# Grouped-query attention on one core: the last pair's transposes, the last V's split and the last norm

## Chip, core and metric

The kernel runs on one core of a Trainium2 chip. The metric is device time in microseconds, the median of several executions. A core has five engines that work side by side, each on its own list of instructions: TensorE (PE, matmuls and transposes), VectorE (DVE), ScalarE (ACT), GpSimd (POOL) and SyncE (SP, which here issues every DMA). They wait for one another by semaphores. Data lies in HBM, is worked on in SBUF (128 partitions), and matmuls write to PSUM.

## What is computed

```python
B, Hq, Hkv, Sq, Sk, D = 16, 32, 8, 16, 2048, 128      # all bfloat16

def reference(q, k, v):
    rep = Hq // Hkv                                    # 4
    k = jnp.repeat(k, rep, axis=1)
    v = jnp.repeat(v, rep, axis=1)
    scores = jnp.einsum("bhqd,bhkd->bhqk", q, k) * D ** -0.5
    p = softmax(scores, axis=-1)
    return jnp.einsum("bhqk,bhkd->bhqd", p, v)
```

Four query heads share one K and V head, so for each of 16 x 8 = 128 groups (batch, KV head) there are 4 x 16 = 64 query rows against 2048 keys. K and V are 64 MB each and are read once.

## The kernel before

Two groups make a **pair**: 64 pairs (NP = 64), each with 128 rows of queries, 1 MB of K and 1 MB of V. For each pair p:

- SP loads K(p) (line 175) and V(p) (line 183), `Kn` and `Vb`. V lies as 128 partitions x 2 groups x 16 blocks (J = 16) of 128 values: partition a holds 16 consecutive keys, so a load has rows of 16 x 128 x 2 bytes = 4 KB. There are 6 K buffers and 8 V buffers. V(63) alone is loaded as two halves of 8 blocks (lines 185 to 188), each with a semaphore of its own, `sem_vl[0]` and `sem_vl[1]`.
- VectorE transposes K (line 311, `KT`).
- TensorE makes the scores S(p) (lines 220 and 264, into `S_ps`, four banks of PSUM).
- VectorE scales them and takes their minimum (line 327, `Sneg`, `nbias`, semaphore `sem_max`), and later the reciprocal of the row sums (line 318, `rrec`, `sem_rec`).
- ScalarE takes the exp (line 357, `P`, with the row sums read from an accumulator, `sem_exp`).
- TensorE transposes P in two stages of four (line 276, `ST_ps`, `sem_st`), each evicted to SBUF by ScalarE (line 367, `PT`, `sem_ev`).
- TensorE multiplies by V: PV(p) (lines 292 and 298, 16 blocks; for the last twelve pairs (NFAST) each block is two matmuls, one for each group, so 32 in all; `sem_pv`). For pairs up to 60 the result goes to `O_ps`; for pairs 61, 62 and 63 into the first 128 columns of three different banks of `S_ps` (`o_ap`, line 145), which the last scores have left by then.
- ScalarE multiplies by the reciprocal and writes the output tile: the norm (lines 380 and 384, `O`, `sem_nm`).
- SP stores it (line 200, 32 KB, 256-byte rows, `sem_o`), one of eight output buffers.

**What sets the order.** TensorE and ScalarE work through two lists written out by hand, `pe_prog` and `act_prog` (lines 92 to 138). In the loop at lines 119 to 128 each step p has the scores of pair p+1, PV and norm of pair p-3 (PVLAG = 3) and the transposes of pair p. What follows the loop (lines 129 to 138) is the tail: TensorE has PV(60), PV(61), PV(62), the transposes of pair 63, PV(63); ScalarE has exp(63), norms 60 and 61, norm 62, the two evictions of pair 63, norm 63. SP's order is the loop at lines 202 to 211: the load of V five steps behind that of K, the store twelve behind, so that V(63) is issued after store(55) and then come stores 56 to 63 alone. At the end SP waits for all stores (line 213).

PV(p) waits for the second eviction of its pair (line 280), for its V (line 282; for pair 63 the two semaphores of the halves, at blocks 0 and 8, line 290), and in the last three pairs for VectorE to have read all scores (line 284). The transposes of a pair wait for its exp (line 271) and for a free stage. The norm waits for PV, the reciprocal and a stored output buffer (lines 373 to 376).

## Time and profile before

| what | value |
|---|---|
| median of 3 runs | 345.48 us (345.41 to 345.74) |
| profiled execution, its own time | 346.02 us |
| its span, from the first instruction to the last | 344.1 us |
| granted TensorE clock, mean | 0.999 of full speed |
| HBM read and written | 136.31 MB and 2.10 MB, 402 GB/s over the span |
| traffic from 332 to 334 us | 383 GB/s |
| traffic from 336 to 337 us | 231 GB/s |
| traffic from 340 to 340.5 us | 34 GB/s |

All times inside the execution are microseconds from the start of the span. The page divides the span into 40 slices of 8.6 us, and gives busy shares by slice as digits (9 is 90% or more). A row of the chain of waits or of the timeline has a start, a length, the engine, the line of the kernel, the operation, and how many instructions it merges; "issue" in the chain is time for which the profile shows no instruction that ended it, which can also be a DMA's landing. A row of DMA issues has what is moved, the queue, the count, the size of each and the time from issue to landing.

### The profile page before, as it was taken

Reading aid. Unit: us, or ns where it says so; the run is one execution under the profiler, and the core shown is the slowest. Engines: PE = TensorE matmul, PEld = TensorE weight load, DVE = VectorE, ACT = ScalarE, POOL = GpSimd, SP = SyncE. Lnnn points to the kernel's source line nnn. Section 1 sums busy time; section 2 is a strip of 40 time slices with the busy share of each in tenths; the row PEclk is TensorE's granted clock in tenths of the full one; section 3 lists DMA queues with packets and bytes.
Section 4 is the critical chain, followed back from the end, with each engine's and each line's share of the span. In section 5 each row is a group of like instructions: output and inputs, shape, how many; then the busy total and the mean of one; then the engine's idle time right before and its main releaser. Section 6 shows DMA issues by size and latency. Waiting matters only on the chain.

```text
span 344.1 us, 8217 instructions
## 1 busy us (share of the span) xinstructions
PE 314.5 (91%) x3904; PEld 189.9 (55%) x2880; DVE 297.4 (86%) x320; ACT 292.3 (85%) x405; POOL 30.3 (9%) x15
## 2 busy tenths in 40 slices
PE   0776999999999999999999999999999999888694
PEld 0422575557555655566566656655665566445263
DVE  2279999999899989998899989998999998988930
ACT  1238899999999999999999999999999999987774
POOL 4500004000400004000210004000040000000000
PEclk9999999999999999999999999999999999999999
DMA  7999999999999999999999999999999999999993
GB/s 292 428 415 416 414 412 416 413 414 413 415 416 417 413 415 416 415 419 416 412 417 415 414 415 417 415 418 417 414 415 420 416 412 416 421 414 415 411 380 97
DMA packets 37300, 138.94 MB, mean 404 GB/s; under 512 B 11408, under 2 KB 11408, under 8 KB 29072
## 3 DMA queue, kind: packets, MB, share of 16 engines
q1 hardware_dynamic: 37264, 138.42, 99.3%
q8 instruction: 27, 0.44, 0.5%
q14 instruction: 9, 0.07, 0.1%
HBM read 136.31 MB, written 2.10 MB: 402 GB/s over the span
## 4 chain that ended last, share of the span: by engine, by line
PE 87%; issue 5%; ACT 3%; DVE 2%; DMA 2%; POOL 1%; SPq 0%; ACTq 0%
PE O_ps L292 28%; PE S_ps L264 18%; PE ST_ps L276 16%; PE S_ps L220 16%; PE ST_ps L242 4%; PE O_ps L298 2%; DMA Qn<-in_q_dram 2%; ACT P L357 1%; DVE KT L311 1%; POOL Q L164 1%; DVE Sneg L327 1%; PE S_ps L298 1%; ACT PT L367 1%; ACT QT L347 0%; ACT O L380 0%
## 5 line engine op out<-in xcount | busy, mean ns | idle before, releaser
L327 DVE TENSOR_SCALAR_CACHE_REDUCE Sneg<-S_ps 128x2048 f32<-128x2048 f32 x64 | 146.3, 2286 | 26.7 <-PE S_ps L220 25.3
L357 ACT ACTIVATE P<-Sneg,nbias 128x2048 bf16<-128x2048 f32 x64 | 158.8, 2482 | 7.5 <-DVE Sneg L327 6.1
L311 DVE STREAM_TRANSPOSE KT<-Kn 128x1024 f32<-128x1024 f32 x128 | 150.9, 1219 | 9.6 <-DMA Kn<-in_k_dram 9.4
L264 PE MATMUL S_ps<-KT,QT 32*64 32x512 bf16 x1024 | 104.3, 395 | 5.2 <-DVE Sneg L327 4.4
L220 PE MATMUL S_ps<-KT,QT 32*64 32x512 bf16 x1024 | 102.9, 389 | 0.0
L292 PEld LDWEIGHTS O_ps<-Vb,PT 128*128 128x128 bf16 x832 | 77.2, 98 | 42.3 <-issue 34.1
L292 PE MATMUL O_ps<-Vb,PT 128*128 128x256 bf16 x832 | 99.9, 273 | 0.0
L367 ACT ACTIVATE PT<-ST_ps 128x512 f32<-128x512 f32 x128 | 69.6, 595 | 7.7 <-PE ST_ps L276 6.5
L276 PE MATMUL ST_ps<-ident,P 128*128 128x128 f32 x512 | 70.0, 280 | 1.9 <-ACT P L357 1.9
L264 PEld LDWEIGHTS S_ps<-KT,QT 32*64 32x64 bf16 x1024 | 30.2, 104 | 71.0 <-issue 62.3
L276 PEld LDWEIGHTS ST_ps<-ident,P 128*128 128x128 f32 x512 | 55.6, 142 | 12.0 <-ACT P L357 7.7
L380 ACT ACTIVATE O<-O_ps,rrec 64x128 bf16<-64x128 f32 x104 | 37.7, 363 | 14.2 <-PE O_ps L292 13.4
L164 POOL COPY Q<-Qn 128x4096 bf16<-128x4096 bf16 x8 | 28.8, 3600 | 224.3 <-PE ST_ps L242 181.5
L242 PE MATMUL ST_ps<-ident,Q 128*128 128x128 f32 x128 | 20.4, 291 | 10.1 <-POOL Q L164 10.1
L347 ACT ACTIVATE QT<-ST_ps 128x512 f32<-128x512 f32 x32 | 19.3, 603 | 10.0 <-PE ST_ps L242 10.0
L242 PEld LDWEIGHTS ST_ps<-ident,Q 128*128 128x128 f32 x128 | 16.4, 151 | 10.1 <-issue 10.1
L298 PE MATMUL O_ps<-Vb,PT 128*64 128x128 bf16 x288 | 9.8, 220 | 7.0 <-issue 7.0
L298 PEld LDWEIGHTS O_ps<-Vb,PT 128*64 128x64 bf16 x288 | 8.5, 110 | 12.7 <-issue 12.7
L318 DVE RECIPROCAL rrec<-rowsum 128x1 f32<-128x1 f32 x64 | 10.1, 158 | 3.1 <-ACT P L357 3.1
L357 ACT ACTIVATION_READ_ACCUMULATOR P<-Sneg,nbias 128x1 f32 x64 | 12.2, 191 | 0.0
L384 ACT ACTIVATE O<-O_ps,rrec 128x128 bf16<-128x128 f32 x9 | 3.3, 367 | 6.7 <-PE O_ps L298 6.7
L298 PE MATMUL S_ps<-Vb,PT 128*64 128x128 bf16 x96 | 3.3, 220 | 2.7 <-issue 1.9
(11 smaller groups left out, 12.3 us busy)
## 6 DMA issues: line engine op xcount, KB each, us to landing
Kn<-in_k_dram SPq DMA_DIRECT2D x64, 1024.0 KB, 15.8
Vb<-in_v_dram SPq DMA_DIRECT2D x63, 1024.0 KB, 17.5
Qn<-in_q_dram SPq DMA_DIRECT2D x8, 256.0 KB, 15.2
out_dram<-O SPq DMA_DIRECT2D x64, 32.0 KB, 15.7
Vb<-in_v_dram SPq DMA_DIRECT2D x2, 512.0 KB, 12.3
```

What stands on the lines that cost most here:

```text
L164: gp.tensor_copy(Q4[:, :, :, :, :].rearrange("p j b r x -> p (j b) r x"), src.unsqueeze(2).to_broadcast([128, 16, 4, 64]),).then_inc(sem_q ...
L220: return pe.add_instruction(mybir.InstMatmult(name=nc.get_next_instruction_name(), engine=mybir.EngineType.PE, ins=[pe.lower_ap(rhs), pe.l ...
L242: ins = pe.transpose(dst[:, 128 * j:128 * (j + 1)], src[:, 4 * x + j, b, :], ident4[:, :])
L264: ins = pe.matmul(s_ap, w, x, start=(acc == 0), stop=(acc == 3))
L276: ins = pe.transpose(dst[:, 128 * t:128 * (t + 1)], P[p % 2][:, 128 * x:128 * (x + 1)], ident4[:, :])
L292: ins = pe.matmul(O_ps[:, 0:256], pt[:, j // 2, j % 2, :], Vb[p % NV][:, :, j, :], start=(j == 0), stop=(j == J - 1),)
L298: ins = pe.matmul(o_ap(p)[64 * g:64 * (g + 1), :], pt[:, j // 2, j % 2, 64 * g:64 * (g + 1)], Vb[p % NV][:, g, j, :], start=(j == 0), stop ...
L311: dve.transpose(KT[p % NKT][:, :].rearrange("p (t b e a x) -> p x e t b a", t=J // 2, b=2, e=2, x=2)[:, x, :, :, :, :], Kn[p % NK][:, :].b ...
L327: dve.tensor_scalar(Sneg[p % 2][:, :].rearrange("p (t h x) -> p h t x", t=8, h=2), S_ps[:, :].rearrange("p (h t x) -> p h t x", t=8, h=2), ...
L357: act.activation(P[p % 2][:, :].bitcast(BF16).rearrange("p (n y e) -> p n y e", n=16, e=2), Sneg[p % 2][:, :].rearrange("p (n e y) -> p n ...
L367: act.activation(PT[p % NPT][:, 4 * h:4 * (h + 1), :].rearrange("p t q -> p (t q)"), stage_ap(u), ACT.Copy,).then_inc(sem_ev, 1)
L380: ins = act.activation(Osb[p % NO][rows, :], O_ps[rows, 128 * g:128 * (g + 1)], ACT.Copy, scale=rrec[rows, p:p + 1])
```

## The change

Three edits, all at the end of the work.

- In the hand-written lists the transposes of pair 63, and so their evictions on ScalarE, come before PV(62) and norm 62.
- V(63) is loaded as blocks 0 to 11 and 12 to 15 instead of 0 to 7 and 8 to 15; PV(63) waits for the second semaphore ahead of block 12.
- The norm of pair 63 leaves ScalarE's list. VectorE does it after its last reciprocal, as a `tensor_scalar` that reads PSUM and writes the same output tile, and signals a new semaphore, `sem_nl`, for which SP's last store waits.

```diff
+LASTV = ((0, 12), (12, 16))
...
+    sem_nl = sem("sem_nl")
...
     for p in range(NP - 4, NP - 2):
         norm(p)
+    transposes(NP - 1)
     pv(NP - 2)
     norm(NP - 2)
-    transposes(NP - 1)
     pv(NP - 1)
-    norm(NP - 1)
...
-                for x in range(2):
-                    dst = Vb[s][:, :, 8 * x:8 * (x + 1), :].rearrange("a g j d -> a g (j d)")
-                    src = vf[:, 2 * p:2 * p + 2, 1024 * x:1024 * (x + 1)]
+                for x, (lo, hi) in enumerate(LASTV):
+                    dst = Vb[s][:, :, lo:hi, :].rearrange("a g j d -> a g (j d)")
+                    src = vf[:, 2 * p:2 * p + 2, 128 * lo:128 * hi]
                     sp.dma_start(dst, src).then_inc(sem_vl[x], 16)
...
             def store(p):
                 s = p % NO
-                sp.wait_ge(sem_nm, p + 1)
+                if p < NP - 1:
+                    sp.wait_ge(sem_nm, p + 1)
+                else:
+                    sp.wait_ge(sem_nl, 1)
...
                     for j in range(J):
-                        if p == NP - 1 and j % 8 == 0:
-                            pe.wait_ge(sem_vl[j // 8], 16)
+                        if p == NP - 1:
+                            for x, (lo, _) in enumerate(LASTV):
+                                if j == lo:
+                                    pe.wait_ge(sem_vl[x], 16)
...
             recip(NP - 1)
+            p = NP - 1
+            dve.wait_ge(sem_rec, NP)
+            dve.wait_ge(sem_o[p % NO], 16 * (p // NO))
+            dve.wait_ge(sem_pv, NP)
+            dve.tensor_scalar(Osb[p % NO][:, :], o_ap(p), rrec[:, p:p + 1], None, op0=ALU.mult).then_inc(sem_nl, 1)
```

## Prediction

> **What bounds the kernel now.** I read the page's head first, then the chain of work that ended last over its closing microseconds, then the timeline of the same stretch, and last the DMA issues of the final loads.

> ```profile
> span 344.1 us, 8217 instructions
> PE 314.5 (91%) x3904; PEld 189.9 (55%) x2880; DVE 297.4 (86%) x320; ACT 292.3 (85%) x405; POOL 30.3 (9%) x15
> DMA  7999999999999999999999999999999999999993
> GB/s 292 428 415 416 414 412 416 413 414 413 415 416 417 413 415 416 415 419 416 412 417 415 414 415 417 415 418 417 414 415 420 416 412 416 421 414 415 411 380 97
> ```

> Three engines are near 90%, but the row of DMA shares is nine in every slice but the first and last: some 415 GB/s, never let go. The loads set the pace, and the change touches only what follows the last of them. So the closing stretch is all that counts. Its chain (start, length, what):

> ```profile
> 334.53 0.36 issue
> 334.89 1.08 PE S_ps L298 x32
> 335.97 1.55 issue
> 337.52 1.08 PE S_ps L298 x32
> 338.61 0.60 PE ST_ps L276 x4
> 339.21 0.02 issue
> 339.23 0.48 ACT PT L367
> 339.71 0.01 issue
> 339.73 0.60 ACT PT L367
> 340.33 0.04 issue
> 340.37 1.10 PE S_ps L298 x32
> 341.48 0.02 issue
> 341.50 0.37 ACT O L384
> ```

> From 334.89 on these are PV(61), PV(62), the transposes of pair 63, their two evictions, PV(63) and its norm. The 1.55 us of "issue" ahead of PV(62) need a name. The timeline (start, length, engine, line) tells what was ready meanwhile:

> ```profile
> 334.08 2.46 ACT L357 ACTIVATE P<-Sneg,nbias 128x2048 bf16<-128x2048 f32 x1
> 336.43 0.20 ACT L357 ACTIVATION_READ_ACCUMULATOR P<-Sneg,nbias 128x1 f32 x1
> 336.78 0.38 ACT L384 ACTIVATE O<-S_ps,rrec 128x128 bf16<-128x128 f32 x1
> 338.54 1.09 PE L276 MATMUL ST_ps<-ident,P 128*128 128x128 f32 x8
> ```

> The exp of pair 63 was done at 336.63, and the transposes that need it started at 338.54. They stood in TensorE's queue behind PV(62), which waited for its V. The issues of the loads, each answered for its own stretch (count, size, us to landing):

> ```profile
> Vb<-in_v_dram SPq DMA_DIRECT2D x1, 1024.0 KB, 14.3
> ```

> ```profile
> Vb<-in_v_dram SPq DMA_DIRECT2D x1, 512.0 KB, 12.2
> ```

> ```profile
> Vb<-in_v_dram SPq DMA_DIRECT2D x1, 512.0 KB, 12.5
> ```

> The first is V(62), issued at 323.09: it landed at 337.4, and PV(62) started at 337.52. The others are the halves of V(63), issued at 326.60 and 327.59: landed at 338.8 and 340.1. So PV(63) at 340.37 was released by the evictions, 0.3 us after its last V. That 0.3 us would look like all there is to gain; but PV(63) also began with all its V on the chip, and could have run most of its matmuls ahead of the last piece.

> **The transposes ahead of PV(62).** Nothing is added or removed, three groups change places. The timeline has the transposes of pair 62 at 332.42, 0.05 us after their exp's accumulator read ended (332.16+0.21); so those of pair 63 start at 336.68, 1.86 earlier. ScalarE has the norms of pairs 60 and 61 in front of the evictions, until 336.78+0.38 = 337.16. The first eviction follows the first transpose by 0.69 (338.54 to 339.23), so starts at 337.37, behind those norms; the pair takes 1.08 and ends at 338.45, and PV(63) may follow 0.06 later, at 338.51. PV(62) pays: a group of eight transposes holds TensorE for 1.02 (from 328.12 to 329.14 where scores follow), so it starts at 337.70 instead of 337.52 and leaves TensorE at 338.72. The norm of pair 62 now queues behind the evictions on ScalarE, which is free at 338.45, before PV(62) ends (338.80): it moves by 0.18, and store(62) on SP with it, from 339.0 to 339.2. Nobody but store(63) queues behind that, some 1.7 us later. So neither ScalarE nor TensorE holds PV(63) past 338.72, where it was 340.37. What is late next is its V.

> **V(63) as 12 and 4 blocks.** Two issues as before, 512 rows as before, of 3 KB and 1 KB instead of 2 KB and 2 KB. The halves landed 1.3 us apart, so a quarter is 0.65: twelve blocks land at 338.8+0.65 = 339.45, the last four at 340.1 as now. Rows of 3 KB and 1 KB occur nowhere in the trace. Its packets took 18 ns for 256 B, 84 for 2 KB, 159 for 4 KB and 309 for 8 KB. One bound: 3 KB as 4 KB and 1 KB as 2 KB, 243 ns where two of 2 KB took 168, over 16 rows for each of the 16 DMA engines +1.2 us. The other: 3 KB as 2 KB, 1 KB as 256 B, 102 ns, -1.1 us. The rows lie on a straight line (75 ns for 2 KB more, 150 for 4 KB more), which gives 121.5+46.5 = 168: no change, which I take.

> [...] The halves here came at 512 KB in 1.3 us, 403 GB/s, beside 415 for whole loads, since they stand in a full queue; I go by the row.

> PV(63) then starts at 339.45+0.08 = 339.53 (PV(62) came 0.1 behind its load). Its 32 matmuls take 1.10, 28 ns each with 0.22 for the last. The 24 of the first twelve blocks are issued by 339.53+0.67 = 340.20, and the last four blocks, landed at 340.1, are usable at 340.18: no second wait worth a number. It ends at 340.63 where it ended at 341.47: **0.84 gained**. If the four blocks come later, all of that goes on at once, less 0.02. Of the 0.84, about 0.2 is the split's: with halves PV(63) would wait at its middle until 340.18 and have 16 matmuls left, 15 x 0.028 + 0.22 = 0.64, ending at 340.82.

> **The norm on VectorE.** Removed: ScalarE's 0.37 (L384). Added: one tensor_scalar of 128x128 out of PSUM with a scalar by partition, and a semaphore of its own. VectorE has done its last reciprocal at 336.67+0.16, so it stands at the wait with nothing behind it. Its other wait, for store(55) (issued at 324.33, 13.3 us to landing), is over at 337.6. The trace has no such instruction. Nearest rows: the reciprocal of 128x1, 158 ns, and the tensor_scalar with reduction of 128x2048 out of PSUM, 2286 ns. 128 columns are near the short one; on the line between them it is 158 + 127 x 1.04 = 290 ns. I take 0.29: **0.08 gained**. The ends are 0.16 (0.21 gained) and 2.29 (1.9 lost).

> [...]

> **The store.** SP issued store(63) at 341.9 as ScalarE's norm ended at 341.87, and it took 1.5 us to land; the span ends 0.7 after that. All of it moves along, to an issue at 340.98 and a landing at 342.5.

> **Sum.** 0.84 + 0.08 = 0.92. The profiled execution took 346.02, with 344.1 of span and 1.92 around it: 343.2 and 345.10. It lies 0.54 above the median of the runs, 345.48; the tail scales by next to nothing, so **344.56**, 0.27% faster.

> **Rivals.**
> *The load hides it.* The time of the chain from V's last byte is what it was: V(63) lands later by some tenths because steady traffic ahead of it shifts. For: the last slices' rate falls to 97 GB/s, so a few laggard DMA engines, not the queue, time the last landing, and that wanders. Against: three runs lie within 0.33 us. With the last piece at 340.5, PV(63) waits until 340.58, then eight matmuls, 7 x 0.028 + 0.22 = 0.42: ends at 341.0, gain 0.47+0.08 = 0.55, **344.9**: no change that can be told.

> *The last store runs into the laggards* (slower). Store(62), issued at 339.0 while V(63) was still landing, took 2.7 us, store(63) on an empty queue 1.5. The latter's issue moves from 1.8 us behind V's last landing to 0.9. If that is near enough to cost 2.7, 1.2 is lost and **345.76** results, slower than now. It decides if the backlog outlasts about 341.4. Against: store(62) had landed by 341.8, and the traffic is down to 5 GB/s from 340.5 to 341 and to none after.

> *Dearer rows* (slower). At the bound above, 3 KB as 4 KB and 1 KB as 2 KB, V(63) ends at 341.3; PV(63) ends at 341.3+0.08+0.42 = 341.8, gain -0.33+0.08: **345.73**. It exceeds the present time once the pieces come 0.9 us later than I say.

> *It does not do what it says.* If PV(62) waited for something other than V(62), the transposes ahead of it still help, but if the exp released late (past 338.5) they don't: gain only 0.08 and the split, **345.2**. The exp's row at 336.63 speaks against.

> **How the numbers follow.** My case 0.70; the load hiding it 0.13; the store 0.07; dearer rows 0.06; the last 0.04. What a measurement here can tell from no change is 0.2%, 0.69 us, so faster means below 344.79 and slower above 346.17. My case by itself spans 344.3 to 344.85, with the VectorE operation from 0.16 to 0.4 and the landing off by 0.2; 0.04 of its 0.70 fall within 0.2%, and 0.02 of the second case beyond: faster 0.68. The slow rivals are priced within 0.2%; a store or rows dearer than that, or a VectorE operation near its long end (346.5), make slower 0.07 of their 0.17, and the rest is same, 0.25. The range takes in the load's case and the last one, and leaves out the slow ones and the long end of VectorE's bound, 0.13 and a little: 344.2 to 345.4.

> **What would show it.** Transposes of pair 63 near 336.7, ahead of PV(62) at 337.7; evictions ended by 338.5; PV(63) starting on the landing of the large piece, near 339.5, with at most 0.1 us of idle time before its 25th matmul; a VectorE tensor_scalar near 0.3 us; store(63) issued near 341.0 with 1.5 us to landing. Wrong would be a last V landing past 340.5, a store of over 2 us, or a norm above 0.4.

## The result, and the profile after

| | kernel before | changed kernel |
|---|---|---|
| median of 22 runs each | 345.67 us (345.29 to 346.01) | 345.04 us (344.40 to 345.51) |
| profiled execution, span | 344.1 us | 343.1 us |

The ratio is 0.9982 with a 95% interval of 0.9975 to 0.9988: 0.63 us, or 0.18%, faster (0.4 to 0.9 us by the interval). That is clear of zero and smaller than the 0.92 us that were predicted. Here the changed kernel's runs also cover more, 1.1 us where those of before cover 0.7; in the experiments below the kernel before covers 1.3 to 2.1. The one profiled execution gained 1.0.

The head of the page after, with its rows of DMA share and rate in 40 slices:

```profile
span 343.1 us, 8217 instructions
PE 312.1 (91%) x3904; PEld 189.2 (55%) x2880; DVE 297.6 (87%) x321; ACT 291.8 (85%) x404; POOL 30.3 (9%) x15
DMA  7999999999999999999999999999999999999993
GB/s 294 429 414 415 415 411 413 414 416 417 412 418 419 413 415 417 412 420 415 412 421 414 414 416 416 415 418 417 415 412 419 419 412 420 417 413 418 410 393 126
```

VectorE has one instruction more, ScalarE one less, and the loads run as they did. The chain of waits over the last ten microseconds (start, length, what):

```profile
326.19 12.98 DMA Vb<-in_v_dram
339.17 0.14 issue
339.30 1.10 PE S_ps L304 x32
340.40 0.03 issue
340.43 0.05 DVEq L347
340.48 0.05 issue
340.53 0.35 DVE O L348
```

Where before there were PV(62), transposes and evictions, there is now one load, that of twelve blocks of V(63), issued at 326.19 and landed at 339.17; PV(63) and its norm stand directly behind it. The timeline shows the rest of the new order (start, length, engine, line, and in brackets the idle time before and what ended it):

```profile
336.20 0.20 ACT L368 ACTIVATION_READ_ACCUMULATOR P<-Sneg,nbias 128x1 f32 x1
336.46 1.09 PE L280 MATMUL ST_ps<-ident,P 128*128 128x128 f32 x8 [0.66 <-ACT P L368]
337.15 1.09 ACT L378 ACTIVATE PT<-ST_ps 128x512 f32<-128x512 f32 x2 [0.23 <-PE ST_ps L280]
337.48 1.09 PE L304 MATMUL S_ps<-Vb,PT 128*64 128x128 bf16 x32
339.30 1.09 PE L304 MATMUL S_ps<-Vb,PT 128*64 128x128 bf16 x32 [0.73 <-DMA Vb<-in_v_dram]
340.53 0.35 DVE L348 TENSOR_SCALAR O<-S_ps,rrec 128x128 bf16<-128x128 f32 x1 [3.92 <-PE S_ps L304]
```

The transposes start 0.06 us after the exp, PV(62) follows them without a gap, the evictions are over at 338.24, and PV(63) is one run of 32 matmuls with no second wait. The page's DMA issues (count, size, median us to landing):

```profile
Vb<-in_v_dram SPq DMA_DIRECT2D x1, 768.0 KB, 13.0
Vb<-in_v_dram SPq DMA_DIRECT2D x1, 256.0 KB, 12.5
```

The second piece, issued at 327.4, landed at 339.85, 0.68 behind the first, while the matmuls of the first still ran.

### The profile page after: what moved, and what is told of

Read it like the earlier page. It is cut to its first block, busy times and chain, and to the rows that moved or that the text cites. A ratio compares the mean times of both kernels' runs of the same rounds, so it can differ in the third digit from the quotient of the medians.

```text
span 343.1 us, 8217 instructions
## 1 busy us (share of the span) xinstructions
PE 312.1 (91%) x3904; PEld 189.2 (55%) x2880; DVE 297.6 (87%) x321; ACT 291.8 (85%) x404; POOL 30.3 (9%) x15
## 2 busy tenths in 40 slices
DMA  7999999999999999999999999999999999999993
## 4 chain that ended last, share of the span: by engine, by line
PE 83%; DMA 5%; issue 4%; DVE 3%; ACT 1%; SPq 1%; POOL 1%; DVEq 0%; ACTq 0%
PE O_ps L298 28%; PE S_ps L268 18%; PE S_ps L224 15%; PE ST_ps L280 15%; PE ST_ps L246 5%; DMA Vb<-in_v_dram 4%; DVE KT L317 2%; PE O_ps L304 2%; DMA Qn<-in_q_dram 1%; DVE Sneg L333 1%; POOL Q L165 1%; SPq L204 1%; ACT P L368 1%; SPq L184 0%; PE S_ps L304 0%
## 5 line engine op out<-in xcount | busy, mean ns | idle before, releaser
L298 PEld LDWEIGHTS O_ps<-Vb,PT 128*128 128x128 bf16 x832 | 77.3, 98 | 44.0 <-issue 35.7
L298 PE MATMUL O_ps<-Vb,PT 128*128 128x256 bf16 x832 | 99.9, 273 | 1.5 <-issue 1.5
L280 PE MATMUL ST_ps<-ident,P 128*128 128x128 f32 x512 | 69.0, 278 | 2.8 <-ACT P L368 2.8
L368 ACT ACTIVATION_READ_ACCUMULATOR P<-Sneg,nbias 128x1 f32 x64 | 12.2, 190 | 0.0
L333 DVE DVE_READ_ACCUMULATOR Sneg<-S_ps 128x1 f32 x64 | 5.3, 83 | 0.0
## 6 DMA issues: line engine op xcount, KB each, us to landing
Kn<-in_k_dram SPq DMA_DIRECT2D x64, 1024.0 KB, 15.9
Vb<-in_v_dram SPq DMA_DIRECT2D x63, 1024.0 KB, 17.7
Vb<-in_v_dram SPq DMA_DIRECT2D x1, 256.0 KB, 12.5
```

Source lines behind the costliest of these rows:

```text
L280: ins = pe.transpose(dst[:, 128 * t:128 * (t + 1)], P[p % 2][:, 128 * x:128 * (x + 1)], ident4[:, :])
L298: ins = pe.matmul(O_ps[:, 0:256], pt[:, j // 2, j % 2, :], Vb[p % NV][:, :, j, :], start=(j == 0), stop=(j == J - 1),)
L333: dve.tensor_scalar(Sneg[p % 2][:, :].rearrange("p (t h x) -> p h t x", t=8, h=2), S_ps[:, :].rearrange("p (h t x) -> p h t x", t=8, h=2), ...
L368: act.activation(P[p % 2][:, :].bitcast(BF16).rearrange("p (n y e) -> p n y e", n=16, e=2), Sneg[p % 2][:, :].rearrange("p (n e y) -> p n ...
```

## The experiments

Each kernel ran 9 to 12 times, in between runs of the kernel before on the same chip, in three groups whose medians of before were 345.73, 345.75 and 345.74. Ratios are against these.

### The three edits apart

**The order alone.**

```diff
+    transposes(NP - 1)
     pv(NP - 2)
     norm(NP - 2)
-    transposes(NP - 1)
     pv(NP - 1)
     norm(NP - 1)
```

> The transposes of pair 63 ahead of PV(62) alone; halves of V(63) and the norm on ScalarE as before. My theory (each term as predicted): PV(63) starts when its first half lands, near 338.8, waits at its middle for the second half and ends near 340.8, so 0.65 us less than before. The rival that the landing of V(63) eats the gain, because PV(63) no longer has slack behind it: 0.3 to 0.5 us less, and runs that scatter more than those of before.

Measured: 345.02, 0.71 less, ratio 0.9981 (0.9972 to 0.9989). Its chain:

```profile
327.14 12.51 DMA Vb<-in_v_dram
339.65 0.04 issue
339.69 0.66 PE S_ps L298 x16
340.35 0.02 issue
340.38 0.37 ACT O L384
```

The order gives its 0.65, as far as the runs can tell (0.4 to 1.0 by the interval). PV(63) waits at its middle, as worked out, and only 16 matmuls and the norm follow the last byte of V. Single runs reach from 344.74 to 345.50, as the rival expected; but those of before in this group reach from 345.55 to 347.25, so the width alone decides nothing.

**The split alone.** `LASTV = ((0, 12), (12, 16))` with the old order and the norm on ScalarE.

> V(63) as 12 and 4 blocks alone. My theory: no difference beyond 0.1 us, since PV(63) is released by ScalarE's evictions near 340.4, after both pieces have landed. If rows of 3 KB and 1 KB were dearer or moved the last landing: 0.2 to 0.5 us more.

Measured: 345.68, ratio 0.9996 (0.9985 to 1.0008): nothing, as long as ScalarE's evictions release PV(63) (340.34 in its trace). In the packet records of the changed kernel's trace, which has the same rows, they took 121 ns (3 KB) and 46 ns (1 KB), together 167 where two rows of 2 KB took 168 in the trace of before: on the straight line on which the prediction had put them.

**The norm alone.** The norm of pair 63 on VectorE, with its semaphore; old order, halves.

> The last norm on VectorE alone. As predicted: 0.08 us less. The rival that the trace of the changed kernel suggests (0.13 from PV's end to VectorE's start and 0.35 for the operation, against 0.03 and 0.37 on ScalarE): 0.07 to 0.1 us more. Both may be too small for the interval, so the trace's own rows decide: PV's last matmul to the end of the norm, 0.40 before.

Measured: 345.82, 0.09 more, ratio 1.0000 (0.9992 to 1.0009); the runs can't tell it, the trace can. The end of its chain (DVEq is the wait on PV, an instruction of its own):

```profile
339.60 1.10 PE S_ps L301 x32
340.70 0.03 issue
340.73 0.05 DVEq L344
340.78 0.05 issue
340.82 0.35 DVE O L345
```

From PV's last matmul at 340.70 to the norm's end at 341.17 it is 0.47 us. On ScalarE it was 0.02 to 0.04 to the start and 0.37 for the operation, 0.40. So the move costs 0.07 instead of gaining 0.08, by a longer operation than the straight line gave (0.35, not 0.29) and a start that is 0.1 later.

**Order and split, the norm back on ScalarE.**

> The changed kernel with its last norm back on ScalarE. As predicted: 0.84 us less than before, a little slower than the changed kernel. The rival that VectorE's norm costs: 0.08 faster than the changed kernel, some 0.7 less than before by the runs (which gave the changed kernel 0.62) and PV's end to the norm's end 0.40. The rival that the landing of V(63) eats the gain: the same as the changed kernel, near 0.6 less, and PV(63) waiting between its 24th and 25th matmul.

Measured: 344.90, 0.83 less, ratio 0.9977 (0.9968 to 0.9987): the predicted 0.84 for these two edits. What the split adds to the order, 0.12 by these medians where 0.19 was worked out, is too little for runs like these. The runs scatter from 344.48 to 345.80, and the profiled execution is the longest of them; its trace shows what happened in it.

### What the scatter is

The page after has the clock at full speed to the end. In the profile of order and split it is not. Its stretches of 3.41 us (start:end, length, busy time of PE, PEld, DVE, ACT and POOL, then PE's granted clock, DMA share, GB/s):

```profile
320.51:323.93 3.42, 3.36 (x64) 2.35 (x56) 2.95 (x4) 2.25 (x6) 0.00 (x0) 1.00 1.02 414
323.93:327.34 3.41, 0.94 (x23) 0.24 (x12) 3.41 (x3) 1.89 (x2) 0.00 (x0) 1.00 1.04 407
327.34:330.75 3.41, 3.41 (x40) 2.91 (x35) 0.38 (x3) 0.97 (x2) 0.00 (x0) 0.50 1.03 410
330.75:334.17 3.42, 3.21 (x67) 1.57 (x51) 1.38 (x1) 3.31 (x4) 0.00 (x0) 1.00 1.01 387
```

TensorE was idle most of the second stretch, and its clock was halved over exactly the third. The timeline there:

```profile
327.15 1.78 PE L301 MATMUL O_ps<-Vb,PT 128*64 128x128 bf16 x32 [2.47 <-issue]
328.86 1.97 PE L277 MATMUL ST_ps<-ident,P 128*128 128x128 f32 x8
```

PV(58) had waited 2.47 us for its V; it then took 1.78 us instead of 1.09, and the transposes of pair 61 1.97 instead of 1.09. Everything behind them on TensorE came late, the scores of pair 63 too, and exp(63) ended at 338.19 where it had ended at 336.63. Further down the same trace:

```profile
338.24 1.09 PE L277 MATMUL ST_ps<-ident,P 128*128 128x128 f32 x8 [1.27 <-ACT P L360]
339.27 1.98 PE L301 MATMUL S_ps<-Vb,PT 128*64 128x128 bf16 x64
```

Now TensorE waits for exp(63), and PV(62), whose V had landed near 337.5 (issued at 323.15, with the 14.3 us of the trace of before), waits behind the transposes; then both PVs run in one piece (x64). In the old order's profiled execution the transposes did not start before 338.54, behind PV(62), though exp(63) would have let them start 1.86 us earlier: with that slack a delay of 1.5 would have stayed out of sight. The new order had used it up.

So the theory became: the gain is 0.84 where exp(63) is on time, and less where the clock was halved ahead of it. The next experiments were made for that.

**The changed kernel again.**

> The changed kernel once more, as the measure for the others on the same chip and for a second trace. Theory now: two things took the predicted 0.92 us down to 0.62: the norm on VectorE is a loss, and in part of the executions TensorE's clock is halved for 3.4 us after its idle time ahead of PV(58), so that exp(63) comes 1.5 us late; before, 1.86 us of slack hid that, and the new order has none. Then: some 0.6 us below before, single runs scattering over about 1 us.

Measured: 345.04, 0.71 less, ratio 0.9982 (0.9971 to 0.9993), runs from 344.44 to 345.76. One stretch of 3.41 us at half speed is 0.005 of the mean clock, and some executions have one near the start as well: in the trace of order and split the mean over the first 40 us is 0.96. Of the 33 runs of the changed kernel, here and with the result, the 16 with a granted clock of at least 0.997 have a median of 344.91, the other 17 one of 345.28. The 99 runs of before in the three groups, sorted the same way, have 345.69 (31 runs) and 345.75 (68): a lower clock goes with 0.37 us in the new order and with 0.06 in the old.

The clock isn't all of the scatter. Two of the runs at full clock took 345.27 and 345.48, and the first of them is the profiled one: exp(63) was on time in it (the transposes started at 336.83), and the twelve blocks of V(63) landed late. Of the changed kernel there are three traces, this one, that of the result and that of the last experiment below, all with the clock up to the end. The landing of the large piece, then the wait behind it (this run, then the last experiment):

```profile
326.73 12.80 DMA Vb<-in_v_dram
339.52 0.14 issue
```

```profile
326.85 12.80 DMA Vb<-in_v_dram
339.65 0.14 issue
```

With 339.17 in the trace of the result, the executions took 344.92, 345.27 and 345.41: each 5.75 or 5.76 us more than the landing. So the landing, which differs by 0.48 us among these three, sets their times one to one. The trace of this run again has a norm of 0.35 on VectorE (from 340.88), with 0.13 in front.

**Work in the idle time.** Order and split, norm on ScalarE, and in TensorE's list, ahead of PV(58)'s wait for V, a filler: sixteen matmuls of 256 columns whose result nobody reads.

```diff
+            def filler(n, v):
+                for _ in range(n):
+                    pe.matmul(O_ps[:, 256:512], ident[:, :], Vb[v % NV][:, 0, 0:2, :],
+                              start=True, stop=True, skip_group_check=True)
...
+                    if p == 58:
+                        pe.wait_ge(sem_nm, p)
+                        filler(16, p - 1)
```

> Order and split with the norm on ScalarE, and 16 matmuls of 256 columns (whose result nobody reads) in TensorE's idle time ahead of PV(58), where the clock was halved in the trace of order and split alone. The clock theory: no halving there, the upper half of the runs (345.3 to 345.8) is gone, median near 344.7 and ratio near 0.997. The rival that the scatter comes from the landing of V(63): the same median and scatter as order and split alone, 344.9 and 1.3 us.

Measured: 344.87, 0.88 less, ratio 0.9976 (0.9967 to 0.9984). The median hardly moved against order and split alone (344.90), where 344.7 was expected; the scatter went from 1.32 us (9 runs) to 0.49 (11 runs, 344.49 to 344.98), and the mean from 345.01 to 344.85, a difference within the uncertainty of so few runs. Seven of the eleven have a mean clock of 0.994 or 0.995, and none of them is above 344.98. The stretch that had been idle, and the next:

```profile
324.81:328.23 3.42, 3.10 (x51) 2.60 (x50) 2.80 (x4) 1.33 (x3) 0.00 (x0) 1.00 1.04 407
328.23:331.64 3.41, 3.41 (x70) 1.76 (x52) 0.82 (x1) 3.20 (x4) 0.00 (x0) 1.00 1.05 416
```

**The same filler in the kernel before.**

> The kernel before with the 16 matmuls ahead of PV(58) alone. The slack theory: no difference beyond 0.1 us, since the halved clock was hidden there. If the filler gained by something else, it would gain here too, 0.1 to 0.2.

Measured: 345.80, ratio 1.0003 (0.9992 to 1.0013), runs from 345.43 to 347.17: nothing in the median. The filler has no gain of its own.

### Taking the slack away

**Twelve matmuls ahead of the scores of pair 63**, in both orders, with no filler ahead of PV(58):

```diff
                 elif op[0] == "S":
                     _, p = op
+                    if p == NP - 1:
+                        pe.wait_ge(sem_nm, p - 4)
+                        filler(12, p - 5)
                     pe.wait_ge(sem_kt, 2 * p + 2)
```

> The kernel before with 12 such matmuls ahead of the scores of pair 63, so that exp(63) ends some 1.3 us later. The slack theory: no more than 0.1 us slower, since the transposes of pair 63 stand behind PV(62) for 1.86 us anyway. The rival that the chain of pair 63 sets the end already: 1.3 us slower.

> Order and split with the same 12 matmuls ahead of the scores of pair 63. The slack theory: the transposes wait for exp(63) until near 338.0, PV(62) stands behind them, and PV(63) ends near 341.1: 0.5 us slower than order and split alone, so only 0.3 us below before. The rival that V(63) alone sets the end: no slower than order and split alone, 0.8 below before.

Measured: the kernel before 345.68, ratio 1.0003 (0.9994 to 1.0011), no slower by the median, as the slack theory had it; but three of its eleven runs took 346.10 to 346.48, where two of the 35 of before in this group are above 346.05. No trace shows why. Order and split 344.89, ratio 0.9982 (0.9973 to 0.9991): no slower either, where 0.5 was expected. The dose was too small. In the trace of the kernel before with it, exp(63) ended at 336.90, 0.1 behind the landing of V(62) at 336.8, where it had been 0.8 ahead: 0.9 later, not 1.3, since exp(63) had been waiting on ScalarE for the evictions of pair 62 (it started at 334.08, VectorE was done at 333.47). From these rows I estimate that this costs 0.1 to 0.2 us in the new order, too little to see. The exception fits: the longest run of order and split with the twelve, 346.55, was the profiled one, and in it the clock was halved again (a second, of 346.38, has no trace).

```profile
324.44:327.85 3.41, 1.03 (x36) 0.95 (x32) 3.17 (x4) 1.29 (x2) 0.00 (x0) 1.00 1.03 402
327.85:331.26 3.41, 3.41 (x22) 2.79 (x17) 0.00 (x0) 2.25 (x4) 0.00 (x0) 0.50 1.04 415
```

**Twenty of them, and the filler ahead of PV(58)**, in both orders:

> The kernel before with the 16 matmuls ahead of PV(58), so that the clock stays up, and 20 ahead of the scores of pair 63 (12 had delayed exp(63) by 0.9 us against the landing of V(62), less than meant). The slack theory: exp(63) ends some 1.1 us behind the landing of V(62), just as PV(62) leaves TensorE; no more than 0.15 us slower than before. The rival that the chain of pair 63 always counts: 1.9 us slower.

> The same two additions to order and split. The slack theory: PV(62) waits behind the transposes, PV(63) ends some 1.1 us later than without, near 345.95: slower than the kernel before by 0.2 and than the old order with the same addition. The rival that V(63) alone sets the end: 344.9, as without.

Measured: the kernel before 345.73, ratio 0.9995 (0.9986 to 1.0004); order and split 345.70, ratio 0.9998 (0.9989 to 1.0007). The same delay costs one order nothing and the other 0.83 of its 0.88. It came out level with the old order, not 0.2 slower. The old order's trace, then the new one's:

```profile
337.37 1.08 PE L309 MATMUL S_ps<-Vb,PT 128*64 128x128 bf16 x32 [0.66 <-issue]
337.73 0.20 ACT L368 ACTIVATION_READ_ACCUMULATOR P<-Sneg,nbias 128x1 f32 x1
338.39 1.10 PE L284 MATMUL ST_ps<-ident,P 128*128 128x128 f32 x8
```

```profile
337.93 0.20 ACT L371 ACTIVATION_READ_ACCUMULATOR P<-Sneg,nbias 128x1 f32 x1
338.18 1.09 PE L285 MATMUL ST_ps<-ident,P 128*128 128x128 f32 x8 [1.27 <-ACT P L371]
339.20 1.98 PE L312 MATMUL S_ps<-Vb,PT 128*64 128x128 bf16 x64
```

With the old order TensorE spends the wait for exp(63) on PV(62), and the transposes follow it as if nothing had happened. With the new order it stands still for 1.27 us and does PV(62) afterwards.

### The norm without the scatter

**The changed kernel with the filler ahead of PV(58).**

> The changed kernel with the 16 matmuls ahead of PV(58): against order and split with the same 16 (344.87, scatter 0.5) it prices the norm on VectorE alone. If VectorE's norm is dearer (0.48 from PV's end against 0.41): 344.94. As predicted at first (0.08 less): 344.79. In any case less scatter than the changed kernel's 1.1 to 1.3.

Measured: 345.01 (344.82 to 345.41), ratio 0.9976 (0.9967 to 0.9986). That is 0.14 above the same kernel with the norm on ScalarE (344.87), by medians from two groups of runs; the ratios are alike. Its trace has 0.35 for the norm and 0.13 in front. The traces' landings take out the wandering of the loads. That of order and split with the filler:

```profile
326.29 13.04 DMA Vb<-in_v_dram
339.32 0.14 issue
```

It took 344.98, 5.66 us more than the landing, where the changed kernel's three have 5.75 and 5.76. So the move costs some 0.09 us there, beside the 0.07 of the norm alone; a gain of 0.08 is not to be seen.

The changed kernel gained nothing that can be told from the filler: its mean is 345.03 with it, 345.02 and 345.09 without, its median 345.01 against 345.04 and 345.04.

The best version by the medians is order and split with the norm on ScalarE: 344.90, or 344.87 with the filler. Its lead over the changed kernel, 0.14 to 0.17 us, is within the uncertainty of the runs; what speaks for it is the traces' 0.07 to 0.09.

## Why the prediction was right in its direction, and too large

| step | predicted | profile after | the same, with 0.2 added for a tail that ran earlier |
|---|---|---|---|
| transposes of pair 63 start | 336.68 | 336.46 | 336.7 |
| evictions end | 338.45 | 338.24 | 338.4 |
| PV(62) starts | 337.70 | 337.48 | 337.7 |
| PV(63) starts | 339.53 | 339.30 | 339.5 |
| PV(63) ends | 340.63 | 340.40 | 340.6 |
| norm, from PV's end | 0.03 + 0.29 | 0.13 + 0.35 | |
| last store to landing | 1.5 | 1.4 | |

- **The mechanism was right.** The wait for V(62) had held the transposes; with them ahead, PV(63) hangs on the large piece of V(63) alone. The tail of this execution ran 0.2 earlier as a whole: V(62) landed at 322.88 + 14.3 = 337.2, not 337.4, and exp(63) ended at 336.40, not 336.63. With that put back, every start is within 0.03 us. It is luck of this execution, and 0.2 of its 1.0.
- **Counted from the last byte of V(63)**, the landings fall out. From there to the end of the span it was 4.04 us in the trace of before (landed at 340.09), 3.34 with the order, 3.12 with order, split and filler, and 3.29, 3.27 and 3.27 in the changed kernel's three. The order is worth 0.70 (0.65 predicted), order and split 0.92 (0.84; in that trace the last four blocks landed 0.75 behind the twelve, in the changed kernel's 0.68 to 0.69), all three edits 0.75 to 0.77 where 0.92 was predicted.
- **The order's and the split's terms were right together**: 0.84 predicted, 0.83 and, with the filler, 0.88 measured; the order 0.65 against 0.71, and the split alone nothing, as a wait that something else covers.
- **The norm's term was wrong in sign.** The failing step is "158 + 127 x 1.04 = 290 ns. I take 0.29: **0.08 gained**". The line ran between a tiny operation and a huge one, of different kinds; the operation took 0.351, and the prediction carried ScalarE's 0.03 from PV's end to the start over to VectorE, where it is 0.13. Together 0.07 lost, 0.15 off: as much as was missing just above, in executions with exp(63) on time.
- **A slack was spent without being priced.** The prediction worked out that the transposes could start 1.86 us earlier, and read that from one execution in which exp(63) was on time. The same 1.86 us was the old order's cover against a late exp(63). That the new order pays for a late exp is shown (0.83 us with the twenty matmuls); how often the changed kernel pays is not: none of its three traces has a halved stretch near the end, and the filler moved its runs by no more than their uncertainty. Without the norm's 0.15 the prediction would have been 0.77, and the measured 0.63, 0.71 and, with the filler, 0.73 are each uncertain by 0.2 to 0.4. Whether anything is missing beyond the norm stays open.
- **The base was low.** The 344.56 stood on a median of three runs, 345.48; the 22 runs of before with the result have 345.67. Of the 0.48 between 344.56 and the 345.04 measured, 0.19 is that. By the prediction's own lines 345.04 is "same", to which it gave 0.25, and not "faster", to which it gave 0.68.
- **Of the rivals**, the load did not hide the gain: in all three traces PV(63) is one run of 32 matmuls without a second wait. The rival's gain of 0.55 came nearer to the measured 0.63 than the 0.92 did, but not by its mechanism; the wandering landing that it named is in the scatter. The last store took 1.4 us, and the rows of 3 KB and 1 KB cost what the line said. None of them priced a late exp that the new order alone pays for. "If the exp released late (past 338.5)" stood in the last one as a condition, with the exp's row of one execution as the answer to it; its 345.2 also gave the split a gain that the split alone did not have.

## What to carry to other kernels

When work moves ahead of a wait on an in-order engine, the wait doesn't vanish: whatever is now behind the moved work waits for that work's own inputs (here TensorE stood still for 1.27 us). Measure the slack that the old order gave those inputs, and ask how often they are late by that much, not in one execution but over many. A wider scatter alone does not tell that a cover has been used up, since the landing of the last load moves the times as well (by 0.48 us among three traces here); runs that sort by the suspected cause in one order and not in the other, as they did here by the clock, are a sign of it, and a delay put in on purpose shows it. And price a small operation on another engine with its start, from the event that releases it to its first cycle (here 0.13 us on VectorE and 0.02 to 0.04 on ScalarE), not by its length alone.

## What the runs showed of the hardware that was not expected

```profile
319.58:322.99 3.41, 2.29 (x44) 1.95 (x44) 3.12 (x4) 2.02 (x5) 0.00 (x0) 1.00 1.03 418
322.99:326.40 3.41, 1.77 (x32) 0.41 (x12) 3.22 (x3) 2.97 (x4) 0.00 (x0) 1.00 1.03 405
326.40:329.82 3.42, 2.72 (x52) 2.03 (x48) 1.41 (x3) 1.38 (x4) 0.00 (x0) 1.00 1.03 409
```

  Here 1.77 of 3.41 us, 52%, was enough. The least that was enough in the traces of before and after is 1.65 us (48%), from 18.86 to 22.27 us in the trace after. The last stretch of before, from 340.06 to 343.47, had 1.09 us (32%), and the clock was at half behind it, with no work left on TensorE. So, as far as these traces show, whether an execution loses 1.5 us on TensorE depends on where the grid lies.
- **The last load comes in over 6.5 us.** In the trace of the kernel before, the sixteen DMA engines finished their shares of the second half of V(63) between 333.6 and 340.1 us; in the trace after those of its two pieces between 332.7 and 339.2 and between 333.3 and 339.85, 6.5 us each. PV(63) waits for the slowest. In the kernel before six of the sixteen were done by 334.84, and from 336 to 337 us the DMA share was 0.62 and the rate 231 GB/s, with the last V still to come. The shares of the second half came 1.26 to 1.33 us behind those of the first, one by one in order of time, and the traffic from 338.5 to 340 us was 44 to 104 GB/s: the prediction's 403 GB/s in a full queue is not what moved when the halves landed. No run here tried to even that out.
